# Fused attention and expert routing: attention's masks built first, more warm-up matmuls, the second q scaled in two halves, the sink gates planned later, and attention's order planned anew

## The chip, the cores and the metric

The kernel runs on one core of a Trainium2 chip. The metric is the device time of one execution in microseconds. Three runs of the kernel before are given, and beside them one profiled execution, from which all rows below come.

## The reference

The program is causal window attention followed by a mixture of experts. Shapes: 4 batches, 8 heads, 768 positions, 64 values per head; 3072 tokens of 512 values, 8 experts with 1024 hidden units.

```python
keep   = (pos < 4) | ((rel >= 0) & (rel < 128))       # rel = query position - key position
scores = where(keep, q @ k.T / 8, -1e9)
a      = exp(scores - max(scores)); a = a / (sum(a) + 1e-9)
x      = (a @ v), heads side by side                  # 3072 x 512
logits = x @ w_gate                                   # 3072 x 8
# greedy over all logits from the largest down: a token goes to its first expert
# that has fewer than 3072 / 8 = 384 tokens
out[tokens of e] = relu(x[tokens of e] @ w1[e]) @ w2[e]
```

## The kernel before

**Stages.** Attention runs first, over 24 chunks of 128 queries (4 batches of 6 blocks); it writes x to device memory and the logits into the tile `L`. Then the routing finds by counting, digit by digit, which tokens each expert takes, and each expert's tokens are gathered and go through the two matrix products. The change touches attention alone, and where the masks are made.

**One chunk of attention.** Chunk c needs its q (transposed, 64 values of two heads on the 128 partitions), its k behind the four sink keys, and its v. The steps, with the planner's names that the diff uses:

- q is scaled by 1/8: `qs` on GpSimd for a whole chunk (L74, called for one tile of 128x512), and `qs.0`, `qs.1`, `qs.2` on VectorE for the three pieces (heads 1/4, 1/4, 1/2) in which chunk 0 is loaded.
- `QK0` to `QK3` (L81, TensorE): scores of one head pair each, 260 columns (132 in the first block of a batch), two matmuls each in the program.
- `cp` (L86 to L88, VectorE): a predicated copy puts the sink and masked values in place. In the first block of a batch it writes `big` (-1e9) where the mask `m0` says so.
- `mx` (L91, VectorE) takes the negated maxima, `e` (L96, ScalarE) the exponentials with their sums.
- `T0`, `T1` (L102, TensorE) transpose the probabilities, `pe` (L103, ScalarE) copies them out, `A` and `B` (L104, L105, GpSimd) cut them to the window.
- `ss`, `sl` (L108, L109), `Ts` (L114), `pS` (L115): the probabilities of the sink keys, split in two parts, transposed and copied out.
- `AV0`, `AV1` (L122, TensorE): probabilities times v; `ae` (L129, VectorE) copies the result out.
- `X0`, `X1` (L137, L140, TensorE): the sinks' part, and the product that puts x and the gate's logits side by side; `xe` (L142, VectorE) divides by the sums and writes `xt`, `lm` (L144, VectorE) adds the logits up into `L`, and SyncE stores `xt` (L145).

**Sink gates.** `X0` multiplies the sink probabilities by a table `vx` that holds the sinks' values and their gate products. The table is made once, in the stretch of chunks 0 and 1: `U` (L62, TensorE, matmuls of 8 columns on the table `us`), `Uc` (ScalarE), `Us` (L67, TensorE, matmuls of 8 columns), `Ud` (L68, VectorE), then `vh` (L69), `vl` (L70), `vx` and `vy` (both L71, VectorE).

**Loads.** Tiles are loaded by DMAs that are issued on SP's queue and, for the q of chunks 0 and 1, on ScalarE's: the three pieces of chunk 0 with k and q in turn, then the identity and the q of chunk 1, then k and q of chunks 1 and 2, v of chunk 0, the sink tables, k and q of chunk 3. From then on a chunk's last score pair is followed by the loads of the chunk four ahead.

**Warm-ups.** `WARM0` matmuls of 512 columns on constants (L53) start TensorE; further ones, called `fill` (L151), stand where the planner sees TensorE idle for more than 400 ns.

**Masks.** GpSimd's queue begins with the routing's constants, written by the constructor of `Moe`. Behind them, in `attention`, stand the masks `mprev` and `m0` and the tile `big`, and behind these the scalings of q and the window cuts.

**Order.** No scheduler acts at run time: each engine runs its instructions in the order in which they are written. That order comes from a planner in the program. `table` lists each step with its engine, its cost in ns and the steps that it depends on; `buffers` says which tiles a step holds and until when; `schedule` plays this through and, on each engine, takes the ready step with the smallest priority, which is the chunk's number times a period plus an offset from the table `OFF`, among those that can start within a window of the earliest. `FIRST` holds the landing times that it assumes for the first loads, `COLD` the time up to which it takes TensorE's steps as 1.6 times as long, `SWITCH` what it adds between kinds of TensorE steps. Steps named `pr0` to `pr16` are the first part of the routing (L497 to L515 and the comparison L490, all on VectorE), done for the first 21 chunks beside the last three.

Of the kernel before, what the change touches and what calls it, by code (L numbers as in the profile page):

```python
# [15 lines left out]
def attention(ctx,tc,qd,kd,vd,vs,ud,pd,iwd,ident,idn,x_dram,L,side={}):  # L16
# [29 lines left out]
    mprev=tl([128,128],"mprev",I32); m0=tl([128,128],"m0",I32); one=tl([128,128],"one",I32); big=tl([128,128],"big")  # L46
    G.memset(one,1)
    for m in (mprev,m0): G.affine_select(m,one,[[1,128]],OP.is_gt,0,base=0,channel_multiplier=-1)
    G.memset(m0[:,0:4],1); G.memset(big,-1.0e9)
    m1=mprev[:,0:4]  # L50
# [23 lines left out]
    def op_qs(c,h=slice(0,HP),e=G): e.tensor_scalar(qs[c%NQ][:,h],qs[c%NQ][:,h],0.125,None,op0=OP.mult)  # L74
    def op_QK(c,g):

        i=c%NB; q=qs[c%NQ]; sp=T('p',c,f'QK{g}')
        k0=(i-1)*W+4 if i else 0; n=260 if i else 132
        for s in range(2):
            p=slice(64*s,64*s+64)  # L80
            PE.matmul(sp[:,s,:n],q[p,g,:],kk[p,g,k0:k0+n],start=True,stop=True)  # L81
# [75 lines left out]
UC=549; WARM0=5  # L157
# [32 lines left out]
def table(cfg):  # L190
# [5 lines left out]
    add('qs','P',lambda c: 1450 if c else None,[('ldq',0)])  # L196
    for h in range(4):
        add(f'QK{h}','E',lambda c: 435 if c%NB else 225,[('ldk',0),('ldk',-1),('qs',0),(f'qs.{min(h,2)}',0),(f'ldk{min(h,2)}',0)]+([(f'~QK{j}',-1) for j in range(3)] if h==3 else []))
        add(f'cp{h}','V',lambda c: 550 if c%NB==1 else 345,[(f'QK{h}',0)])
        add(f'mx{h}','V',344,[(f'cp{h}',0)])  # L200
        add(f'e{h}','A',697,[(f'mx{h}',0)])
# [12 lines left out]
    add('U','E',f0(860),[('ldu',0)])  # L214
# [34 lines left out]
def schedule(cfg,off,T,nb=NC,dl={}):  # L249
# [7 lines left out]
    for c in range(nb):  # L257
        for k,(e,cost,deps) in o.items():
            n=0
            for x,dc in deps:  # L260
                cc=c+dc
                if cc<0 or (dc<0 and cc//NB!=c//NB and x[0]!='~') or (x[0]=='^' and c==0): continue
                x=x.strip('~^')
                rdeps[x,cc].append((k,c)); n+=1
            nd[k,c]=n; ready[k,c]=0.0
# [92 lines left out]
COLD=6500  # L358
# [9 lines left out]
OFF={'A0': 15034, 'A1': 45179, 'AV0': 23765, 'AV1': 17217, 'B0': -9280, 'B1': -53066, 'QK0': -5907, 'QK1': -3388, 'QK2': -3032, 'QK3': -253, 'T0': 7878, 'T1': 10234, 'Ts': -92291, 'U': -35159, 'Uc': -39381, 'Ud': -42332, 'Us': 19706, 'X0': 32667, 'X1': 39254, 'ae0': 217110, 'ae1': -115057, 'cp0': -4377, 'cp1': 13457, 'cp2': -230461, 'cp3': -47449, 'e0': -61344, 'e1': 24247, 'e2': 10856, 'e3': 484225, 'lm': -15093, 'mx0': 32807, 'mx1': -73387, 'mx2': -8086, 'mx3': -51448, 'pS': -31001, 'pe0': -33445, 'pe1': -52676, 'pr0': -44011, 'pr1': 105836, 'pr10': 134063, 'pr11': 484687, 'pr12': -32310, 'pr13': 141140, 'pr14': 249747, 'pr15': 315275, 'pr16': 8621, 'pr2': -37615, 'pr3': 8456, 'pr4': -5323, 'pr5': -137567, 'pr6': -42400, 'pr7': 48263, 'pr8': 10969, 'pr9': 44553, 'qs': -85908, 'r': -21269, 'ra': 253505, 'sl': 96619, 'ss': 8175, 'vh': 287446, 'vl': 59670, 'vx': 316495, 'vy': 137937, 'xe': -83812, 'xo': -18776}  # L368
# [4 lines left out]
DL={}  # L373
# [483 lines left out]
def attention_moe(tc,qd,kd,vd,iwd,ident,w1,w2,out,n_sink,window,vs=None,ud=None,pd=None):  # L857
    nc=tc.nc
    with ExitStack() as ctx:
# [26 lines left out]
```

## Time and profile before

| what | value |
|---|---|
| three runs | 493.31, 495.43, 497.24 us; median 495.43 |
| profiled execution | 497.0 us, of which its span on the core is 495.3 |
| mean clock granted to TensorE in it | 0.968 |
| attention | from the start to about 155 us |
| routing and experts | from there to the end |

How to read it: the span begins with the first instruction of the core and ends with the last; the times of all rows are counted from its start. Where a line of the program holds one matmul of 4-byte values, the profile counts two or four for it, so the counts of its rows stand above those of the order. Rows that name a chain follow the execution back from its last instruction; a row of a timeline gives in brackets how long the engine stood idle ahead of it, and what ended that. Matmuls overlap, so that the mean duration of one is longer than the busy time divided by their count.

### The profile page before, as it was taken

Reading aid. Unit: us, or ns where it says so; the run is one execution under the profiler, and the core shown is the slowest. Engines: PE = TensorE matmul, PEld = TensorE weight load, DVE = VectorE, ACT = ScalarE, POOL = GpSimd, SP = SyncE. Lnnn points to the kernel's source line nnn. Section 1 sums busy time; section 2 is a strip of 40 time slices with the busy share of each in tenths; the row PEclk is TensorE's granted clock in tenths of the full one; section 3 lists DMA queues with packets and bytes.
Section 4 is the critical chain, followed back from the end, with each engine's and each line's share of the span. In section 5 each row is a group of like instructions: output and inputs, shape, how many; then the busy total and the mean of one; then the engine's idle time right before and its main releaser. Section 6 shows DMA issues by size and latency. Waiting matters only on the chain.

```text
span 495.3 us, 11327 instructions
## 1 busy us (share of the span) xinstructions
PE 468.7 (95%) x4147; PEld 386.4 (78%) x4147; DVE 379.8 (77%) x1147; ACT 234.0 (47%) x672; POOL 148.4 (30%) x212
## 2 busy tenths in 40 slices
PE   8999999999997698999989999999999999999994
PEld 4878787787786367867867877887888887998983
DVE  5699989899998687998989989999999374531210
ACT  4578887777870044344344353363523365522110
POOL 6667575665642010041022030301302142002001
PEclk9999999999998587999999999999999999999998
DMA  8656666766322171473562551745725674601001
GB/s 266 194 159 187 174 191 176 192 201 174 106 66 65 49 254 63 143 233 136 164 199 106 169 193 59 253 138 183 221 83 161 224 250 133 214 0 44 21 22 43
DMA packets 75464, 73.13 MB, mean 148 GB/s; under 512 B 28560, under 2 KB 57872, under 8 KB 75408
## 3 DMA queue, kind: packets, MB, share of 16 engines
q1 hardware_dynamic: 70992, 59.29, 39.7%
q0 software_dynamic: 3840, 12.59, 7.2%
q8 instruction: 33, 0.54, 0.4%
q10 hardware_dynamic: 576, 0.52, 0.4%
q14 instruction: 23, 0.19, 0.1%
HBM read 59.80 MB, written 12.58 MB: 146 GB/s over the span
## 4 chain that ended last, share of the span: by engine, by line
PE 61%; DVE 22%; DMA 8%; issue 4%; POOL 2%; ACT 1%; POOLq 0%; SPq 0%; DVEq 0%; ACTq 0%
PE ph L738 20%; PE py L751 15%; PE pp L81 8%; PE pp L122 6%; DVE wl L692 4%; PE pp L140 3%; DMA xg<-x_dram,idx 3%; DVE cmp L490 2%; DMA raw<-w 2%; PE pp L102 2%; DVE hl L743 2%; PE pr L562 2%; DMA out<-yo,idx 1%; DMA kk<-kd 1%; PE pt L704 1%
## 5 line engine op out<-in xcount | busy, mean ns | idle before, releaser
L690 ACT ACTIVATE wh<-raw 128x1024 fp32r<-128x1024 f32 x64 | 67.3, 1059 | 73.8 <-DMA raw<-w 46.4
L738 PE MATMUL ph<-xh,wh 128*128 128x384 f32 x256 | 92.1, 360 | 0.7 <-DVE hl L743 0.7
L692 DVE TENSOR_TENSOR wl<-raw,wh 128x1024 fp32r<-128x1024 f32 x64 | 77.9, 1218 | 12.9 <-ACT wh L690 12.5
L738 PE MATMUL ph<-xh,wl 128*128 128x384 f32 x256 | 87.1, 340 | 0.0
L738 PE MATMUL ph<-xl,wh 128*128 128x384 f32 x256 | 86.7, 342 | 0.2 <-DVE xl L727 0.2
L751 PE MATMUL py<-wh,hh 128*128 128x512 f32 x192 | 78.8, 411 | 0.0
L751 PE MATMUL py<-wl,hh 128*128 128x512 f32 x192 | 75.5, 393 | 0.0
L751 PE MATMUL py<-wh,hl 128*128 128x512 f32 x192 | 75.4, 393 | 0.0
L742 ACT ACTIVATE hh<-ph 128x384 fp32r<-128x384 f32 x64 | 31.3, 490 | 90.5 <-PE ph L738 82.0
L96 ACT ACTIVATE P<-pp,nmx 128x132 f32<-128x132 f32 x192 | 68.7, 371 | 9.1 <-DVE nmx L91 8.0
L756 POOL DMA_INDIRECT out<-yo,idx x24 | 24.9, 1038 | 153.6 <-ACT yo L754 119.5
L697 POOL DMA_INDIRECT xg<-x_dram,idx x24 | 29.0, 1209 | 123.1 <-DVE mx L505 34.2
L743 DVE SCALAR_TENSOR_TENSOR hl<-ph,hh 128x384 fp32r<-128x384 f32 x64 | 34.3, 549 | 39.3 <-ACT hh L742 39.2
L81 PE MATMUL pp<-kk,q 64*128 64x260 f32 (+1 forms) x384 | 61.1, 421 | 2.5 <-ACT P L96 1.0
L738 PEld LDWEIGHTS ph<-xh,wh 128*128 128x128 f32 x256 | 49.0, 192 | 4.3 <-DVE hl L743 2.2
L738 PEld LDWEIGHTS ph<-xh,wl 128*128 128x128 f32 x256 | 49.0, 192 | 1.2
L738 PEld LDWEIGHTS ph<-xl,wh 128*128 128x128 f32 x256 | 48.7, 191 | 0.7 <-DVE xl L727 0.5
L81 PEld LDWEIGHTS pp<-kk,q 64*128 64x128 f32 x384 | 33.9, 207 | 14.8 <-ACT P L96 7.5
L751 PEld LDWEIGHTS py<-wh,hl 128*128 128x128 f32 x192 | 36.0, 188 | 8.0
L91 DVE TENSOR_REDUCE nmx<-pp 128x2 f32<-128x264 f32 x96 | 39.8, 426 | 1.0
L751 PEld LDWEIGHTS py<-wh,hh 128*128 128x128 f32 x192 | 36.2, 188 | 5.2 <-ACT yo L754 0.2
L103 ACT ACTIVATE PT<-pp 128x512 f32<-128x512 f32 x48 | 28.7, 597 | 24.0 <-PE pp L102 19.8
(173 smaller groups left out, 824.6 us busy)
## 6 DMA issues: line engine op xcount, KB each, us to landing
raw<-w SPq DMA_DIRECT2D x64, 512.0 KB, 4.2
v<-vd SPq DMA_DIRECT2D x24, 256.0 KB, 3.3
x_dram<-xt SPq DMA_DIRECT2D x24, 256.0 KB, 3.0
kk<-kd SPq DMA_DIRECT2D x23, 264.0 KB, 4.2
q<-qd SPq DMA_DIRECT2D x22, 256.0 KB, 3.9
xg<-x_dram,idx POOLq DMA_INDIRECT x24, 4.0
out<-yo,idx POOLq DMA_INDIRECT x24, 3.2
us<-ud SPq DMA_DIRECT2D x1, 274.5 KB, 5.8
```

The lines of the kernel that those rows point to most:

```text
L81: PE.matmul(sp[:,s,:n],q[p,g,:],kk[p,g,k0:k0+n],start=True,stop=True)
L91: V.tensor_reduce(T('nmx',c)[:,2*g:2*g+2],sp[:,:,o:o+132],AX.X,OP.max,negate=True)
L96: A.activation(T('P',c)[:,4*s+g,:],sp[:,s,o:o+132],AF.Exp,bias=T('nmx',c)[:,h:h+1],scale=1.0,accum_out=T('sm',c)[:,h:h+1])
L103: def op_pe(c,g): A.activation(T('PT',c)[:,4*g:4*g+4,:].rearrange("p j (s n)->p s j n",s=2),T('p',c,f'T{g}')[:,:,0:256].rearrange("p s (j ...
L122: mm=PE.matmul(av[64*s:64*s+64,hp-2*g,:],T('v',j)[:,h*64:h*64+64],T(x,c)[:,h,:],start=hp==2*g and x=='A',stop=x=='B' or not i,skip_group_c ...
L690: g.add('A',947,lambda wh=wh,raw=raw: nc.scalar.activation(wh,raw,AF.Copy),[f'raw{n%4}'],[f'wh{s}'],f'H{k}.{j}',f'W{k}')
L692: g.add(e,{'V':1135,'P':2303}[e],lambda wh=wh,wl=wl,raw=raw,e=e: (nc.vector if e=='V' else nc.gpsimd).tensor_tensor(wl,raw,wh.bitcast(F32) ...
L697: g.add('P',1450,lambda t=t: nc.gpsimd.indirect_dma_start(out=self.xg[t],out_offset=None,in_=self.x_dram,in_offset=bass.IndirectOffsetOnAx ...
L738: for c,i in part: nc.tensor.matmul(p[:,0:CAP],three[i][0][:,c,:],three[i][1][:,c,:],start=n==0 and i==0,stop=last and i==2)
L742: g.add('A',371,lambda f=f,p=p: nc.scalar.activation(self.hh[:,f,:],p[:,0:CAP],AF.Relu),ps,[f'hh{f}'],f'hh{k}.{f}',f'H{k}')
L743: g.add('V',469,lambda f=f,p=p: nc.vector.scalar_tensor_tensor(self.hl[:,f,:],p[:,0:CAP],0.0,self.hh[:,f,:].bitcast(F32),op0=OP.max,op1=OP ...
L751: nc.tensor.matmul(p,x[:,f,ts],w,start=f==0 and i==0,stop=f==7 and i==2)
```

## The change

The masks move into a function of their own that is called before the routing's constants, so that GpSimd makes them first. Seven warm-ups stand at the start instead of five. The q of chunk 1 is scaled by two steps of two head pairs each, `qh0` and `qh1`, instead of one `qs`. In the planner's table `U` now waits for `AV1` of chunk 0, and costs 900; the fourth score pair of chunk 0 waits for `mx1` of chunk 0 (the mark `!` means: for chunk 0 alone); `COLD` is 7300. The table `OFF` has new values, and a table `DL` that was empty gives single steps of the chunks 0 to 2 and 20 to 23 an offset of their own.

```diff
+def attention_masks(nc,pool):
+    G=nc.gpsimd
+    mprev,m0,one=[pool.tile([128,128],I32,name=n) for n in ("mprev","m0","one")]; big=pool.tile([128,128],F32,name="big")
+    G.memset(one,1); G.memset(big,-1.0e9)
+    for m in (m0,mprev): G.affine_select(m,one,[[1,128]],OP.is_gt,0,base=0,channel_multiplier=-1)
+    G.memset(m0[:,0:4],1)
+    return mprev,m0,big
-def attention(ctx,tc,qd,kd,vd,vs,ud,pd,iwd,ident,idn,x_dram,L,side={}):
+def attention(ctx,tc,qd,kd,vd,vs,ud,pd,iwd,ident,idn,x_dram,L,masks,side={}):
...
-    mprev=tl([128,128],"mprev",I32); m0=tl([128,128],"m0",I32); one=tl([128,128],"one",I32); big=tl([128,128],"big")
-    G.memset(one,1)
-    for m in (mprev,m0): G.affine_select(m,one,[[1,128]],OP.is_gt,0,base=0,channel_multiplier=-1)
-    G.memset(m0[:,0:4],1); G.memset(big,-1.0e9)
-    m1=mprev[:,0:4]
+    mprev,m0,big=masks; m1=mprev[:,0:4]
...
+    def op_qh(c,g): op_qs(c,slice(2*g,2*g+2))
...
-UC=549; WARM0=5
+UC=549; WARM0=7
...
-    add('qs','P',lambda c: 1450 if c else None,[('ldq',0)])
+    add('qs','P',lambda c: 1450 if c>1 else None,[('ldq',0)])
+    for g in range(2): add(f'qh{g}','P',lambda c: 760 if c==1 else None,[('ldq',0)])
     for h in range(4):
-        add(f'QK{h}','E',lambda c: 435 if c%NB else 225,[('ldk',0),('ldk',-1),('qs',0),(f'qs.{min(h,2)}',0),(f'ldk{min(h,2)}',0)]+([(f'~QK{j}',-1) for j in range(3)] if h==3 else []))
+        add(f'QK{h}','E',lambda c: 435 if c%NB else 225,[('ldk',0),('ldk',-1),('qs',0),(f'qh{h//2}',0)]+([('!mx1',0)] if h==3 else [])+[(f'qs.{min(h,2)}',0),(f'ldk{min(h,2)}',0)]+([(f'~QK{j}',-1) for j in range(3)] if h==3 else []))
...
-    add('U','E',f0(860),[('ldu',0)])
+    add('U','E',f0(900),[('ldu',0),('AV1',0)])
...
-                if cc<0 or (dc<0 and cc//NB!=c//NB and x[0]!='~') or (x[0]=='^' and c==0): continue
-                x=x.strip('~^')
+                if cc<0 or (dc<0 and cc//NB!=c//NB and x[0]!='~') or (x[0]=='^' and c==0) or (x[0]=='!' and c): continue
+                x=x.strip('~^!')
...
-COLD=6500
+COLD=7300
...
+        masks=attention_masks(nc,top)
         m=Moe(ctx,tc,L,idn)
...
-            if n_sink==4 and window==128: attention(actx,tc,qd,kd,vd,vs,ud,pd,iwd,ident,idn,x_dram,L,m.side())
+            if n_sink==4 and window==128: attention(actx,tc,qd,kd,vd,vs,ud,pd,iwd,ident,idn,x_dram,L,masks,m.side())
```

Of the table `OFF` two entries show the kind of change: `'U': -35159` becomes `'U': -33562`, and `'Us': 19706` becomes `'Us': 1705`. Of `DL`, two are `'QK1@2': -6625` and `'T0@2': 8815`.

After the change the lines stand three to five further down: L62 becomes L65, L74 L77, L81 L85, L102 L106, L122 L126, L142 L146, L144 L148, L151 L155, and those of the routing from L490 on stand five further down.

**VectorE at its start.** The names are the q tile of chunk 0 (`q_0`), the score tiles (`pp`), the mask `m0` and the tile `big`, and the maxima (`nmx`). Before:

```order
L74 TENSOR_SCALAR q_0_181<-q_0_181 128x128 x2
L88 COPY_PREDICATED pp3_230<-m0_219,big_221 128x2x128
L74 TENSOR_SCALAR q_0_181<-q_0_181 128x256
L88 COPY_PREDICATED pp2_229<-m0_219,big_221 128x2x128
L91 TENSOR_REDUCE nmx_3_242<-pp3_230 128x2
```

After:

```order
L77 TENSOR_SCALAR q_0_190<-q_0_190 128x128 x2
L77 TENSOR_SCALAR q_0_190<-q_0_190 128x256
L92 COPY_PREDICATED pp3_230<-m0_64,big_66 128x2x128
L92 COPY_PREDICATED pp2_229<-m0_64,big_66 128x2x128
L95 TENSOR_REDUCE nmx_3_244<-pp3_230 128x2
```

The scaling of the third q piece (128x256) moves ahead of the first predicated copy.

**TensorE from the last scores of chunk 0 on.** `q_1` and `q_2` in a row are the q of the chunks 1 and 2, `idt` the identity of the transposes, `us` the table that L62 reads, `pk` the one that L67 reads, `A` and `v` the operands of A·V. Before:

```order
L81 MATMUL pp3_230<-kk_180,q_1_182 128x260 x2
L102 MATMUL pp2_229<-idt_62,P_2_238 128x64 x8
L81 MATMUL pp1_228<-kk_180,q_1_182 128x260 x2
L81 MATMUL pp0_227<-kk_180,q_1_182 128x260 x2
L62 MATMUL pp2_229<-us_186 128x8 x4
L102 MATMUL pp3_230<-idt_62,P_2_238 128x64 x8
L81 MATMUL pp2_229<-kk_180,q_1_182 128x260 x2
L114 MATMUL pp1_228<-idt_62,ss_2_258 128x64 x2
L81 MATMUL pp3_230<-kk_180,q_2_183 128x260 x2
L67 MATMUL pp1_228<-U_188,pk_187 128x8 x4
```

After:

```order
L85 MATMUL pp3_230<-kk_189,q_1_191 128x260 x2
L106 MATMUL pp2_229<-idt_62,P_2_240 128x64 x8
L85 MATMUL pp1_228<-kk_189,q_1_191 128x260 x2
L106 MATMUL pp0_227<-idt_62,P_2_240 128x64 x8
L85 MATMUL pp2_229<-kk_189,q_2_192 128x260 x2
L85 MATMUL pp3_230<-kk_189,q_2_192 128x260 x2
L85 MATMUL pp0_227<-kk_189,q_1_191 128x260 x2
L106 MATMUL pp1_228<-idt_62,P_1_239 128x64 x8
L85 MATMUL pp2_229<-kk_189,q_1_191 128x260 x2
L85 MATMUL pp1_228<-kk_189,q_2_192 128x260 x2
L126 MATMUL pp3_230<-A_2_254,v_4_216 64x128 x8
L65 MATMUL pp0_227<-us_195 128x8 x4
```

L62, which stood ahead of the second transpose of chunk 0, now stands behind the first A·V. The two transposes (L106) have one score pair between them. Ahead of this place the further warm-ups move: before, L151 issues two between the second and the third score pair of chunk 0; after, L155 issues four between the third and the fourth.

**VectorE in the last chunks.** `di`, `s`, `oh`, `w`, `mx`, `xb0`, `v`, `vm` and `f` are tiles of the routing's first part, `at` the copies of A·V, `ss` the split sink probabilities, `xt` the tile that is stored, `L` the logits. Before:

```order
L91 TENSOR_REDUCE nmx_2_241<-pp1_228 128x2
L511 TENSOR_SCALAR di_112<-s_101 128x21
L507 TENSOR_SCALAR di_112<-s_101 128x21
L506 TENSOR_SCALAR di_112<-s_101 128x21
L509 TENSOR_TENSOR oh_111<-w_110,mx_102 128x168
L508 CAST xb0_107<-di_112 128x42
L512 TENSOR_SCALAR di_112<-s_101 128x21
L129 COPY at_2_268<-pp2_229 128x256
L129 COPY at_1_267<-pp0_227 128x256 x2
L109 TENSOR_TENSOR ss_2_258<-P_1_237,ss_2_258 128x8x8
```

After:

```order
L146 TENSOR_TENSOR xt_2_273<-pp3_230,r_1_265 128x2x4x72
L113 TENSOR_TENSOR ss_1_259<-P_0_238,ss_1_259 128x8x8
L148 TENSOR_REDUCE L_61<-xt_2_273 128x8
L146 TENSOR_TENSOR xt_1_272<-pp0_227,r_0_264 128x2x4x72
L502 TENSOR_REDUCE v_107<-L_61 128x21
L148 TENSOR_REDUCE L_61<-xt_1_272 128x8
L506 TENSOR_TENSOR w_119<-L_61,v_107 128x168
L504 TENSOR_TENSOR vm_108<-pen_103,v_107 128x21
L133 COPY at_2_270<-pp1_228 128x256
L507 TENSOR_SCALAR f_109<-vm_108 128x21
L508 TENSOR_TENSOR w_119<-w_119,rev_95 128x168
```

Before, a run of routing steps stood ahead of the copies of A·V and of the split; after, the split stands ahead of the first routing step, and the copies come sooner among those steps.

## Rows read from the trace of the kernel before

**Rows 1.** Windows by stage, all engines: length, busy us of each engine, granted clock, DMA.

```profile
9.00:19.00 10.00, 10.00 (x64) 7.96 (x62) 6.93 (x23) 6.79 (x32) 5.63 (x5) 1.00 1.10 349
...
27.00:151.00 124.00, 120.42 (x1766) 99.78 (x1763) 117.46 (x347) 95.11 (x418) 75.26 (x99) 1.00 0.59 162
...
156.00:177.00 21.00, 15.36 (x188) 8.80 (x189) 15.58 (x79) 2.11 (x2) 4.99 (x11) 0.51 0.30 90
```

**Rows 2.** Timeline of VectorE, the last L144 of attention: start us, us, instruction, idle.

```profile
154.74 0.27 DVE L144 TENSOR_REDUCE L<-xt 128x8 f32<-128x64 f32 x1
```

**Rows 3.** Groups by form, 8 to 22.8 us: count | busy us, mean ns | idle.

```profile
L81 PE MATMUL pp<-kk,q 64*128 64x260 f32 x28 | 7.9, 688 | 0.7 <-DMA kk<-kd 0.7
...
L102 PE MATMUL pp<-idt,P 64*128 64x64 f32 x32 | 2.7, 318 | 0.0
...
L122 PE MATMUL pp<-A,v 128*64 128x128 f32 x16 | 2.0, 428 | 0.0
...
L62 PE MATMUL pp<-us 128*128 128x8 f32 x8 | 1.9, 363 | 0.0
```

**Rows 4.** The same view, 27 to 151 us.

```profile
L81 PE MATMUL pp<-kk,q 64*128 64x260 f32 x276 | 43.2, 412 | 0.1
...
L102 PE MATMUL pp<-idt,P 64*128 64x64 f32 x342 | 18.0, 223 | 1.2 <-DVE xt L142 1.0 <-ACT P L96 0.2
```

**Rows 5.** Chain that ended last: start us, us, what ran or was waited for.

```profile
2.89 5.02 DMA kk<-kd
...
27.47 1.97 PE pp L122 x32
```

**Rows 6.** Timeline of TensorE, the first 23 us.

```profile
0.85 2.29 PE L53 MATMUL pp<-const-float32-0.0 128*128 128x512 bf16 x5 [0.85 <-PEq L879]
3.77 1.29 PE L81 MATMUL pp<-kk,q 64*128 64x132 f32 x8 [0.62 <-DVE q L74]
4.99 1.04 PE L151 MATMUL pp<-const-float32-0.0 128*128 128x512 bf16 x2
...
8.05 1.24 PE L81 MATMUL pp<-kk,q 64*128 64x260 f32 x4 [0.74 <-DMA kk<-kd]
...
20.95 1.97 PE L122 MATMUL pp<-A,v 128*64 128x128 f32 x16
```

**Rows 7.** Line 533 alone: min/median/max ns, first and last start.

```profile
L533 PE MATMUL ph<-onesb x21: 326/527/528, 171.6 to 178.3; 128*128 128x384 bf16 x21
```

**Rows 8.** Timeline of TensorE: warm-up matmuls of the routing stage.

```profile
171.59 5.85 PE L533 MATMUL ph<-onesb 128*128 128x384 bf16 x19
```

**Rows 9.** Timeline of VectorE, the start.

```profile
5.38 0.43 DVE L88 COPY_PREDICATED pp<-m,big 128x256 f32<-128x256 int32 x1 [1.20 <-POOL big L49]
5.72 0.28 DVE L74 TENSOR_SCALAR q<-q 128x256 f32<-128x256 f32 x1
```

**Rows 10.** Timeline of ScalarE with its DMA queue, the start.

```profile
0.82 1.84 ACTq L29 DMA_DIRECT2D q<-qd  x4
```

**Rows 11.** DMA issues of 0 to 3 us: KB each, median us to landing.

```profile
q<-qd ACTq DMA_DIRECT2D x1, 128.0 KB, 3.4
```

**Rows 12.** Timeline of GpSimd, the start.

```profile
6.29 1.50 POOL L74 TENSOR_SCALAR q<-q 128x512 f32<-128x512 f32 x1 [0.94 <-DMA q<-qd]
9.52 1.49 POOL L74 TENSOR_SCALAR q<-q 128x512 f32<-128x512 f32 x1 [1.73 <-DMA q<-qd]
```

**Rows 13.** Timeline of VectorE: the second L142.

```profile
31.95 0.76 DVE L142 TENSOR_TENSOR xt<-pp,r 128x576 f32<-128x576 f32 x1
```

**Rows 14.** VectorE alone, first copy of chunk 1 to that L142: window, busy us.

```profile
9.40:31.95 22.55, 17.80 (x50) 1.00 0.63 192
```

**Rows 15.** Timeline of TensorE, the last chunks.

```profile
147.85 0.40 PE L137 MATMUL pp<-vx,pS 64*128 64x288 f32 x2 [0.30 <-DVE at L129]
...
149.08 0.28 PE L114 MATMUL pp<-idt,ss 64*128 64x64 f32 x2 [0.43 <-DVE ss L109]
```

More of the change, by code (lines that the diff above doesn't have):

```diff
@@ L367, in plan_of @@
     return dict(seq=[(k,c) for _,_,k,c in ev],slot=sl,bufs={t:n for t,(n,_) in buffers(cfg).items()})
-OFF={'A0': 15034, 'A1': 45179, 'AV0': 23765, 'AV1': 17217, 'B0': -9280, 'B1': -53066, 'QK0': -5907, 'QK1': -3388, 'QK2': -3032, 'QK3': -253, 'T0': 7878, 'T1': 10234, 'Ts': -92291, 'U': -35159, 'Uc': -39381, 'Ud': -42332, 'Us': 19706, 'X0': 32667, 'X1': 39254, 'ae0': 217110, 'ae1': -115057, 'cp0': -4377, 'cp1': 13457, 'cp2': -230461, 'cp3': -47449, 'e0': -61344, 'e1': 24247, 'e2': 10856, 'e3': 484225, 'lm': -15093, 'mx0': 32807, 'mx1': -73387, 'mx2': -8086, 'mx3': -51448, 'pS': -31001, 'pe0': -33445, 'pe1': -52676, 'pr0': -44011, 'pr1': 105836, 'pr10': 134063, 'pr11': 484687, 'pr12': -32310, 'pr13': 141140, 'pr14': 249747, 'pr15': 315275, 'pr16': 8621, 'pr2': -37615, 'pr3': 8456, 'pr4': -5323, 'pr5': -137567, 'pr6': -42400, 'pr7': 48263, 'pr8': 10969, 'pr9': 44553, 'qs': -85908, 'r': -21269, 'ra': 253505, 'sl': 96619, 'ss': 8175, 'vh': 287446, 'vl': 59670, 'vx': 316495, 'vy': 137937, 'xe': -83812, 'xo': -18776}
+OFF={'A0': 3566, 'A1': 68904, 'AV0': 23490, 'AV1': -54870, 'B0': 50180, 'B1': -8375, 'QK0': -11402, 'QK1': -6817, 'QK2': -7324, 'QK3': 208, 'T0': 3441, 'T1': 6408, 'Ts': -24063, 'U': -33562, 'Uc': 36180, 'Ud': -33378, 'Us': 1705, 'X0': 28046, 'X1': -11706, 'ae0': 22354, 'ae1': 12933, 'cp0': -60932, 'cp1': -113859, 'cp2': 36173, 'cp3': 118185, 'e0': 14705, 'e1': -236202, 'e2': 42795, 'e3': -147363, 'lm': -69786, 'mx0': -207103, 'mx1': -20852, 'mx2': -175794, 'mx3': -57270, 'pS': 13167, 'pe0': 628292, 'pe1': -41356, 'pr0': 14452, 'pr1': 10874, 'pr10': 26429, 'pr11': 67741, 'pr12': 103900, 'pr13': 35733, 'pr14': 58646, 'pr15': -237999, 'pr16': -37794, 'pr2': -22384, 'pr3': 21144, 'pr4': 36050, 'pr5': 132677, 'pr6': 622285, 'pr7': 201632, 'pr8': -14661, 'pr9': 1836, 'qh0': 0, 'qh1': 3896, 'qs': 45199, 'r': 564000, 'ra': 435238, 'sl': 421755, 'ss': 732629, 'vh': 49536, 'vl': 108950, 'vx': -6186, 'vy': 779306, 'xe': -58979, 'xo': 107970}
 PCFG={'win': 80, 'ae': 'V'}
```

2 lines of the change are left out of this document (1 added, 1 removed).

## Prediction

> **What bounds the kernel now.** I read the stages first. TensorE is busy 120.4 of 124 us between 27 and 151 us and VectorE 117.5, so attention, which ends at 155.0 us (154.74 + 0.27), is bound by both together [rows 1, 2]. The change touches nothing behind it but the time at which it ends. I then looked for a stage in which the same work takes longer, and compared groups by form. From 8 to 22.8 us 28 score matmuls of 260 columns keep TensorE busy for 7.9 us (0.282 each), against 43.2 for 276 (0.157 each) later on; transposes take 0.084 against 0.053 [rows 3, 4]. The 16 matmuls of the first A·V take 1.97 us; later 32 of them take 1.97 [rows 5, 6].
>
> So TensorE runs at the lower of its two levels (1.2 GHz) until about 23 us. The clock column does not say so: it shows 1.00 there, though nothing ran at that speed. The durations do: five warm-ups of 512 columns in 2.29 us are about 1.1 columns per ns, and the same 384-column matmul takes 527 ns in a stretch at a granted 0.51 and 326 at full clock [rows 1, 6, 7]. That is what the change can win back. What did TensorE do before a rise? From 171.6 us on it ran 19 warm-ups without a break, and came out fast [rows 7, 8]. At about 23 us it had run scores, transposes and the first A·V in one piece [rows 6]. What did not raise it: 0.85 to 8 us, with breaks of 0.62 and 0.74, and 8 to 19 us, without a break, but with sixteen matmuls of the sink gates in it (8 columns each, 1.9 us for every eight) [rows 1, 3, 6].
>
> The Trainium skill ("TensorE: Matmul & The Clock Gate", Part 1) says that the array starts throttled and that sustained matmul activity releases it. The trace disagrees with that as it stands: TensorE is busy 10.00 of 10 us from 9 to 19 and stays slow [rows 1, 3]. By the rule alone nothing would be left to win there, and the sum would be the rival "nothing but the tail" below, 496.5.
>
> **The change, part by part.** The profiled execution took 497.0 us, its span 495.3; the sum is made against 497.0. That is 1.6 above the median of the runs shown, 495.43, and inside their spread.
>
> *Masks first.* VectorE waited 1.20 us for `big` and made its first predicated copy at 5.38 [rows 9]. Now GpSimd writes the masks before the routing's constants, which nobody reads until the last chunks. But the order also puts the scaling of the third q piece ahead of that copy on VectorE. Its DMA is the third of four issued within 1.84 us from 0.82 on, so at about 1.73, and lands 3.4 later, at 5.1 [rows 10, 11]. With 0.28 for the scaling [rows 9] the copy starts at about 5.4, as before: **0.0** (bounds -0.1 and +0.3). A transfer takes the place of the wait. Behind that copy in VectorE's queue stand the other copies of chunk 0, for which the exponentials wait; they keep their times.
>
> *Seven warm-ups, and four later.* Two more at 0.46 (2.29/5) fill the break of 0.62 in front of the first scores; the first two pairs end at about 5.3. The two warm-ups that stood at 4.99 are gone from there, so a break of some 0.3 opens before the third pair, which needs the scaling that ends at 5.4. Four (1.8 us) now stand between the third and the fourth pair, about 6.3 to 8.1 [rows 6]. They lie over the wait for k of chunk 1, issued at 2.89 and landing at 7.9 [rows 5], so they cost nothing; if that transfer came earlier, up to 1.8. What then breaks the stretch before the first A·V is the 0.3 and perhaps a moment before q of chunk 2, whose scaling on GpSimd ends at 9.52 + 1.49 = 11.0 [rows 12].
>
> *q in halves.* The first half would be ready at 6.29 + 0.75 = 7.04 instead of 7.79 [rows 12]; k comes at 7.9, so **0.0**. SP's queue keeps its loads; only the first two stores of xt move, and nobody waits for them before the routing.
>
> *Sink gates later.* Line 62's matmuls move behind the first A·V, line 67's further still. The first L142 now waits for them together with more of the score work, but the second L142, which stood at 31.95 us, has the same steps ahead of it in both orders on TensorE, and on VectorE the same 46 but for one tiny one [rows 13]. I take that instruction as the mark.
>
> *What the clock gives back.* If the upper level comes by about 8 to 11 us instead of 23, TensorE saves: scores 7.9 - 28 x 0.157 = 3.5; transposes 2.7 - 32 x 0.053 = 1.0; A·V 2.0 - 1.0 = 1.0; sink gates, of which no row shows the upper level, between 0 and half of 3.8, and by the ratio of the scores (0.157/0.282) 1.7. Sum 7.2, bounds 5.5 and 7.4 [rows 3 to 6]. Not all of it can come back. VectorE is in order and has 17.80 us of work from the first copy of chunk 1 at 9.40 to the mark [rows 14]; that copy waits for k of chunk 1 and cannot come earlier. With no idle time the mark would stand at 27.2 (4.75 won); with the share of 117.5/124 that VectorE reaches in the steady stretch [rows 1] it takes 18.8, so 28.2: 3.8 won. The early chunks have more waits, not fewer, so I take the latter: **-3.8**, bounds 0 and -4.75 by this row, -7.2 if VectorE's time shrank too.
>
> *The middle of attention.* From chunk 4 on the plan swaps neighbours (a third score pair ahead of a second and the like) at a pace that the same two engines set: **0.0**, bounds -1 and +1, the size by which 120.4 and 124 leave room [rows 1].
>
> *The last chunks.* Before, steps of the routing's preparation stood ahead of the copies of A·V and of the split of the sink weights on VectorE, and TensorE waited 0.30 and 0.43 for them [rows 15]. Now the split stands ahead of the first of them, the two copies of one chunk have two or three of them ahead instead of six, and the eight ahead of the next copy lie beside the A·V that this copy waits for. **-0.5**, bounds 0 and -0.7.
>
> Sum: 497.0 - 3.8 - 0.5 = 492.7.
>
> **Rivals.** *The clock rises only behind the first A·V.* For it: that is what stood ahead of the rise before [rows 6]; against it: eleven warm-ups now stand in the first 8 us with hardly a break, and warm-ups alone did it at 171.6 [rows 8]. Then seven score groups, three transposes and A·V are as slow as before, and only the sink gates and one transpose gain: 1.7 + 0.25, with the tail 2.4 in all: 494.6. The Trainium skill ("TensorE: Matmul & The Clock Gate", Part 4: PE-mode transpose) says that transposes do not count towards the clock as matmuls do; two of them now stand close together early, one score pair apart. That would make this rival likelier; no row here shows transposes alone.
>
> *All of it comes back.* VectorE's 17.80 us hold instructions stretched by waits for GpSimd, and a different order may shed them: 497.0 - 7.2 - 0.5 = 489.3.
>
> *Slower: the sink gates right behind A·V.* The stretch that raised the clock before ran on from A·V into scores. Now line 62's matmuls of 8 columns follow A·V at once, and line 67's after a few groups. If the early warm-ups do not raise the clock and this breaks the later stretch, it stays low through the second A·V: four more score groups (4 x 4 x 0.125 = 2.0) and 32 matmuls of A·V (2.0) are slow. 497.0 + 4.0 - 0.5 = 500.5. It decides from the moment at which the first A·V ends at the lower level.
>
> *Nothing but the tail.* Part of the spread of the runs before may be a clock that sometimes rose early; if it does not rise earlier now, 496.5.
>
> **How the numbers follow.** About 1%, 5 us, is what a measurement of this kernel can tell from no change, that is below 490.5 or above 500.4. Forecast 0.58, with its own range 491.2 to 494.2; behind A·V 0.20; all back 0.12; slower 0.06; tail alone 0.04. The range 489.4 to 496.5 takes in all but the slower case and the fringe of "all back". Faster by over 1%: the 0.12 and 0.05 of the forecast's lower fringe, 0.17; slower 0.05; the rest 0.78.
>
> **What would show it.** In the changed profile: the first predicated copy at 5.4 with no wait for `big` but with one for a q DMA; score groups of about 0.157 us per matmul from 11 us on; line 62 behind the first A·V; the second L142 near 28 us; the last L144 ending near 150.7; no wait of TensorE for lines 129 and 109 in the last chunks. The forecast is wrong if scores are still at 0.28 us each at 15 us, or if the second L142 stands where I say and the end of attention does not follow it.

## The result, and the profile after

The changed kernel takes 490.33 us (median of 20 runs, 486.83 to 493.6) against 495.32 (20 runs, 491.52 to 498.22): a ratio of 0.9907, 95% interval 0.9881 to 0.9933, so 3.3 to 5.9 us. 490.33 lies in the stated range, 489.4 to 496.5, though under the forecast's own, 491.2 to 494.2. The ratio is that of the means of the runs within 1.5% of the fastest of their kernel, here and below, and so differs a little from the quotient of the medians, which are of all runs. The middle of the ratio is just under 1% faster, the case that had 0.78; the median, 490.33, is just below the 490.5 of the case that had 0.17. The result lies on the line between the two.

The profiled execution took 491.29 us, its span 489.6. The stages, with the columns of [rows 1]:

```profile
9.00:19.00 10.00, 8.69 (x90) 5.88 (x91) 8.88 (x27) 7.77 (x39) 7.63 (x8) 1.00 1.08 341
...
27.00:149.00 122.00, 118.74 (x1741) 98.27 (x1738) 113.95 (x337) 92.10 (x408) 73.71 (x99) 1.00 0.59 160
```

The steady stretch runs as before: TensorE is busy 118.7 of 122 us, before 120.4 of 124 [rows 1]. What changed lies ahead of it. The groups by form of the same 8 to 22.8 us as in [rows 3]:

```profile
L85 PE MATMUL pp<-kk,q 64*128 64x260 f32 x44 | 6.9, 422 | 0.4 <-ACT P L100 0.3
...
L65 PE MATMUL pp<-us 128*128 128x8 f32 x8 | 1.1, 259 | 0.0
```

44 score matmuls take 6.9 us there, 0.157 each, which is the figure of [rows 4] and not the 0.282 of [rows 3]; the eight of the sink gates take 1.1 us instead of 1.9. The timeline of TensorE, beside [rows 6]:

```profile
0.85 3.15 PE L56 MATMUL pp<-const-float32-0.0 128*128 128x512 bf16 x7 [0.85 <-PEq L885]
...
6.19 0.81 PE L85 MATMUL pp<-kk,q 64*128 64x132 f32 x4 [1.01 <-DVE pp L92]
6.93 1.89 PE L155 MATMUL pp<-const-float32-0.0 128*128 128x512 bf16 x4
8.75 1.44 PE L85 MATMUL pp<-kk,q 64*128 64x132 f32 x8
...
10.27 0.66 PE L85 MATMUL pp<-kk,q 64*128 64x260 f32 x4
...
16.11 1.09 PE L126 MATMUL pp<-A,v 128*64 128x128 f32 x16
17.14 1.06 PE L65 MATMUL pp<-us 128*128 128x8 f32 x8
```

Up to 9.8 us the lower level (1.2 GHz) still shows: four matmuls of 132 columns take 0.81 us and the four later warm-ups 1.89. From 10.27 a score group takes 0.66, the first A·V 1.09 instead of 1.97, and the sink gates stand behind it. The trace's records of the granted clock begin at 9.8 us, before at 23.3. The timeline of VectorE:

```profile
5.14 0.30 DVE L77 TENSOR_SCALAR q<-q 128x256 f32<-128x256 f32 x1 [1.22 <-DMA q<-qd]
5.35 0.76 DVE L92 COPY_PREDICATED pp<-m,big 128x256 f32<-128x256 int32 x2
...
9.61 0.43 DVE L92 COPY_PREDICATED pp<-m,big 128x256 f32<-128x256 int32 x1 [1.67 <-PE pp L85]
...
10.43 0.42 DVE L90 COPY_PREDICATED pp<-mprev,pp 128x256 f32<-128x256 int32 x1
...
28.60 0.75 DVE L146 TENSOR_TENSOR xt<-pp,r 128x576 f32<-128x576 f32 x1
...
151.93 0.43 DVE L148 TENSOR_REDUCE L<-xt 128x8 f32<-128x64 f32 x2
```

The first predicated copy starts at 5.35 behind the scaling of the third q piece, which waited 1.22 us for its DMA; `big` holds nobody. Up to 9.61 VectorE sat idle for 1.67 us until the last scores of chunk 0 came, and those stood behind the four warm-ups; the first copy of chunk 1 followed at 10.43. The second L146 stands at 28.60 (31.95 in [rows 13]), 3.35 us earlier; the last L148 ends at 152.36 (155.01 by [rows 2]), 2.65 earlier. The profiled pair differs by 5.7 us, so 3.05 of them arise behind attention. There the code is the same. Windows of the routing and the first expert, before and then after, clock in the third column from the right:

```profile
187.10:194.00 6.90, 6.07 (x24) 5.66 (x25) 5.59 (x16) 4.08 (x6) 0.00 (x0) 0.51 0.24 80
194.00:201.00 7.00, 7.00 (x48) 5.97 (x48) 5.58 (x18) 0.49 (x1) 0.00 (x0) 1.00 0.01 2
```

```profile
184.00:191.00 7.00, 6.21 (x43) 5.43 (x44) 6.70 (x21) 4.30 (x7) 0.00 (x0) 1.00 0.29 79
191.00:198.00 7.00, 6.92 (x47) 5.69 (x46) 6.48 (x22) 0.98 (x2) 0.00 (x0) 1.00 0.17 61
```

The kernel before fell to the lower level once more, from 187.1 to 194.0 us, with the first expert's matrix products under way; the changed one did not. That this goes by chance and not by the kernel, the six profiles of whole kernels suggest (the last two columns from the timelines and the records of the granted clock):

| kernel | from the last logits step to the end, us | at the lower level in it, up to 300 us |
|---|---|---|
| changed, gates early | 335.4 | 17.1 |
| before, two warm-ups | 336.1 | 20.5 |
| before, gates late | 336.6 | 23.9 |
| changed | 337.2 | 20.5 |
| before | 340.3 | 27.3 |
| changed, no late warm-ups | 342.1 | 30.7 |

The same code takes 335 to 342 us there, in the main longer the longer the clock is low, and the two kernels stand on both sides. So eight of the experiments leave routing and experts out.

### The profile page after: what moved, and what is told of

Read it like the earlier page. It is cut to its first block, busy times and chain, and to the rows that moved or that the text cites. A ratio compares the mean times of both kernels' runs of the same rounds, so it can differ in the third digit from the quotient of the medians.

```text
span 489.6 us, 11364 instructions
## 1 busy us (share of the span) xinstructions
PE 462.1 (94%) x4151; PEld 379.3 (77%) x4151; DVE 377.9 (77%) x1147; ACT 233.3 (48%) x672; POOL 148.6 (30%) x213
## 4 chain that ended last, share of the span: by engine, by line
PE 55%; DVE 27%; DMA 7%; issue 5%; ACT 3%; POOL 1%; POOLq 0%; ACTq 0%; DVEq 0%; SPq 0%
PE ph L743 18%; PE py L756 16%; PE pp L85 6%; PE pp L126 5%; DVE wl L697 4%; DMA xg<-x_dram,idx 4%; DVE cmp L495 3%; PE pp L144 2%; ACT P L100 2%; DVE nmx L95 2%; DVE hl L748 2%; DVE pp L90 2%; PE pp L106 2%; PE pr L567 2%; POOL xg L702 1%
## 5 line engine op out<-in xcount | busy, mean ns | idle before, releaser
L743 PE MATMUL ph<-xh,wh 128*128 128x384 f32 x256 | 90.8, 355 | 0.7 <-DVE hl L748 0.6
L743 PE MATMUL ph<-xh,wl 128*128 128x384 f32 x256 | 86.1, 336 | 0.0
L702 POOL DMA_INDIRECT xg<-x_dram,idx x24 | 29.0, 1208 | 120.4 <-DVE mx L510 31.3
L85 PE MATMUL pp<-kk,q 64*128 64x260 f32 (+1 forms) x384 | 57.6, 403 | 2.6 <-ACT P L100 1.3
L85 PEld LDWEIGHTS pp<-kk,q 64*128 64x128 f32 x384 | 32.1, 195 | 14.7 <-ACT P L100 8.2
L108 POOL TENSOR_SCALAR_AFFINE_SELECT A<-PT 128x512 f32<-128x512 f32 x48 | 30.4, 636 | 38.7 <-ACT PT L107 38.6
```

The costliest lines, as they stand in the source:

```text
L108: def op_A(c,g): G.affine_select(T('A',c)[:,4*g:4*g+4],T('PT',c)[:,4*g:4*g+4],[[0,4],[1,128]],OP.is_ge,0.0,base=0,channel_multiplier=-1)
L702: g.add('P',1450,lambda t=t: nc.gpsimd.indirect_dma_start(out=self.xg[t],out_offset=None,in_=self.x_dram,in_offset=bass.IndirectOffsetOnAx ...
L743: for c,i in part: nc.tensor.matmul(p[:,0:CAP],three[i][0][:,c,:],three[i][1][:,c,:],start=n==0 and i==0,stop=last and i==2)
```

## The experiments

Times are medians with range and count. The first four are whole kernels, beside 35 runs of the kernel before with a median of 495.14.

**1. The kernel before with two more warm-ups ahead of chunk 1.**

```diff
+            if (k,c)==('QK0',1):
+                for j in range(2): PE.matmul(T('p',1,'QK0')[:,0,:],wz[:,0:128],wz,start=True,stop=True)
             ops[k[:-1]](c,int(k[-1]))
```

> The kernel before, with two more warm-up matmuls of 512 columns between the last score pair of chunk 0 and the first of chunk 1, so that TensorE runs without a break from the fills at 4.99 us to the sink gates at about 11.5; nothing else. Theory (the clock came back early because warm-ups and scores ran without a break ahead of the sink gates, and that is most of the gain): score matmuls at 0.157 us each before 12 us, the second L142 at 28.5 to 29.5 us instead of 31.95, attention ending 2.5 to 3.5 us earlier, the time 2 to 4 us below before. Rival (the order is the gain, the sink gates' place above all): the clock still rises near 23 us, the second L142 at about 32, the time within 1 us of before.

494.37 us (489.21 to 497.65, 12), ratio 0.9974 (0.9936 to 1.0012). The timeline of TensorE:

```profile
7.66 1.01 PE L157 MATMUL pp<-const-float32-0.0 128*128 128x512 bf16 x2 [0.34 <-ACT P L96]
...
12.04 1.87 PE L62 MATMUL pp<-us 128*128 128x8 f32 x8
...
21.50 1.97 PE L122 MATMUL pp<-A,v 128*64 128x128 f32 x16
```

The theory fell. TensorE ran without a break from 7.66 on, and the gates (1.87) and the first A·V at 21.50 (1.97) are as slow as in [rows 3, 6]; the second L142 stands at 32.55, the level rose at 23.9, and the time is within 1 us of before, as the rival said. In this profile an unbroken stretch that soon holds the sink gates did not bring the level.

**2. The changed kernel without the four later warm-ups.**

```diff
-            for j in range(c[1]): PE.matmul(d,wz[:,0:128],wz,start=True,stop=True)
+            for j in range(0): PE.matmul(d,wz[:,0:128],wz,start=True,stop=True)
```

> The changed kernel without the four warm-ups of L155 between the third and the fourth score pair of chunk 0; the seven at the start stay. Theory (these four close the break in which TensorE waited for k of chunk 1, and so bring the upper level at 9.8): the breaks are open again, the level comes behind 12 us, the second L146 stands at 29.5 to 31 us instead of 28.60, the time 1 to 3 us above the changed kernel. Rival (the seven at the start do it): scores at 0.157 us from 10 us on, the second L146 at 28.6, the time as that of the changed kernel.

492.64 us (488.62 to 495.48, 12), ratio to before 0.9955 (0.9922 to 0.9987), 2.3 above the changed kernel. Timeline and windows:

```profile
3.93 0.72 PE L85 MATMUL pp<-kk,q 64*128 64x132 f32 x8
...
7.52 1.24 PE L85 MATMUL pp<-kk,q 64*128 64x260 f32 x4 [1.68 <-POOL q L77]
```

```profile
3.90:7.30 3.40, 1.47 (x17) 1.05 (x16) 2.68 (x8) 1.41 (x9) 2.16 (x20) 1.00 1.04 312
7.30:10.80 3.50, 3.28 (x26) 2.70 (x28) 2.50 (x9) 2.97 (x15) 3.29 (x5) 0.51 1.08 368
```

Both theories were half right. In this profile seven warm-ups alone had the level up by 3.9 us: eight matmuls of 132 columns take 0.72 instead of 1.29 [rows 6]. Then TensorE sat idle for 1.68 us, and from 7.3 to 10.8 the clock is down again. Here the four would have had to hold the level, not to raise it; in the changed kernel's own profile it came only behind them, at 9.8, so that they may also raise it. Their absence also let chunk 1 start at 7.52: the second L146 stood at 26.63, and the last L148 ended at 148.69, 3.67 earlier than in the profile with them. The routing then took the 342.1 of the table. So the 2.3 of the medians can hold some of the routing's scatter; experiment 7 leaves the routing out.

**3. The kernel before with the gates behind the first A·V.**

```diff
-    add('U','E',f0(860),[('ldu',0)])
+    add('U','E',f0(860),[('ldu',0),('AV1',0)])
```

> The kernel before with one edit of the planner's table: the sink gates' first step waits for the first A.V; warm-ups and masks as before, the order otherwise nearly that of before. Theory (the early sink gates, matmuls of 8 columns, were what kept TensorE at the lower level through 11 to 20 us): the level rises between 11 and 16 us, the second L142 at 29 to 30.5, the time 1 to 3 us below before. Rival (only warm-ups in the first 10 us bring the early rise): rise near 23 us as before, the second L142 at 31.5 to 32.5, the time within 1 us of before. Slower by 3 to 4 us if the gates behind A.V keep the level low.

495.25 us (493.14 to 498.24, 12), ratio 1.0022 (0.9988 to 1.0056). The timeline of TensorE:

```profile
13.69 0.53 PE L102 MATMUL pp<-idt,P 64*128 64x64 f32 x8
...
17.13 1.09 PE L122 MATMUL pp<-A,v 128*64 128x128 f32 x16
```

With five warm-ups as before, the level did rise sooner, at 13.9 (a transpose group of 0.53 us at 13.69, A·V in 1.09), and the second L142 stood at 29.30, 2.65 earlier, both as the theory had it. Nothing of it arrived: the last L144 begins at 155.2, before at 154.74 [rows 2]. Experiment 11 takes that up.

**4. The changed kernel with the gates early.**

```diff
-    add('U','E',f0(900),[('ldu',0),('AV1',0)])
+    add('U','E',f0(900),[('ldu',0)])
```

> The changed kernel with one edit of the planner's table undone: the sink gates' first step no longer waits for the first A.V, so that it stands ahead of the second block of scores again; warm-ups, masks and halves as changed. Theory (the level is up at 9.8, ahead of the gates in either place): no change of level, the gates at about half of their 1.9 us, the second L146 within 0.7 us of 28.6, the time within 1 us of the changed kernel. Rival (the place of the gates is what is won): the level low until about 20 us, the second L146 at 31 or later, the time 2 to 4 us above the changed kernel.

492.12 us (490.99 to 495.87, 12), ratio to before 0.9976 (0.9947 to 1.0005), 1.8 above the changed kernel, between the two theories' figures. In its profile the level stayed up, the first eight matmuls of the gates took 1.03 us and the second L146 stood at 28.13, as the theory said. The loss is at the end: this edit of the table also moved steps of the last chunks. VectorE there, this kernel and then the changed one:

```profile
150.10 0.85 DVE L495 TENSOR_TENSOR cmp<-xb,row 128x1344 bf16<-128x1344 bf16 x1
150.86 0.32 DVE L514 TENSOR_TENSOR oh<-w,mx 128x168 bf16<-128x168 f32 x1
151.11 0.74 DVE L133 COPY at<-pp 128x256 f32<-128x256 f32 x2
...
153.53 0.27 DVE L148 TENSOR_REDUCE L<-xt 128x8 f32<-128x64 f32 x1
```

```profile
148.69 0.41 DVE L133 COPY at<-pp 128x256 f32<-128x256 f32 x1
149.02 0.85 DVE L495 TENSOR_TENSOR cmp<-xb,row 128x1344 bf16<-128x1344 bf16 x1
149.79 0.42 DVE L133 COPY at<-pp 128x256 f32<-128x256 f32 x1
```

The copies of the last A·V (L133) stand at 151.11 behind the routing steps L510, L495 and L514, together 1.3 us; in the changed kernel one stands ahead of the long comparison and one behind it. From the 18th L148 to the last it takes 31.04 us against 29.36.

**5 to 8. Attention alone.** The cut is the same in all of these and the last four:

```diff
-        m.pools(ctx,w1,w2,x_dram,out)
-        with tc.manual_schedule(engines=set(ENGS[:5])): m.run()
+        nc.sync.dma_start(out[0:128,0:NC*E],L.rearrange("p c e->p (c e)"))
```

> The kernel before, cut off behind attention: routing and experts are left out, and in their place the logits tile is stored into the first rows of the output. Attention is unchanged. It measures attention alone, 156 to 160 us by the profile before (155.0 us, the store and what lies around the span), in many runs. Theory (the scatter of the whole kernel, 490 to 499 us, comes mostly from the clock in the routing, which is left out here): the runs lie within 4 us of each other. Rival (it comes from attention): they scatter by 6 us or more.

> The changed kernel, cut off behind attention in the same way: routing and experts are left out. Theory A (the whole 5 us of the medians are won in attention): its median 4 to 5.5 us below that of the kernel before cut in the same way. Theory B (the profiled pair is typical, attention wins about 2.65 and the rest of that pair's difference was the clock in the routing): 2 to 3.3 us below.

> The changed kernel cut off behind attention (routing and experts are left out), without the four warm-ups of L155. Theory (they cost nothing and hold the clock up): its median 1 to 3 us above the changed kernel cut in the same way. Rival (they push the first scores of chunk 1 from 7.5 to 9.4 us, as in its profile, and the clock comes back anyway): 1 to 3 us below it.

Its edit is that of experiment 2. The last of the four:

```diff
-    for i in range(WARM0): PE.matmul(pp[0][:,0],wz[:,0:128],wz,start=True,stop=True)
+    for i in range(WARM0+2): PE.matmul(pp[0][:,0],wz[:,0:128],wz,start=True,stop=True)
```

> The kernel before cut off behind attention (routing and experts are left out), with seven warm-ups at the start instead of five and its own order otherwise. Theory (seven at the start alone can bring the upper level at about 4 us, and the early order does not matter for it): its median 2 to 4 us below the kernel before cut in the same way. Rival (the breaks and the sink gates behind them bring the lower level back, or it never comes): within 0.7 us of it, the scores at 0.28 us each at 15 us.

| cut kernel | median us (range, runs) | level up by | second L142/L146 |
|---|---|---|---|
| 5, before | 159.99 (157.47 to 161.52, 6) | 20.6 | 30.97 |
| 6, changed | 156.50 (155.22 to 157.54, 6) | 9.3 | 27.93 |
| 7, changed, no late warm-ups | 157.57 (157.24 to 158.36, 6) | 4.9, then down 8.3 to 15.1 | 28.03 |
| 8, before, seven warm-ups | 159.22 (158.0 to 162.13, 6) | 4.4, then twice down | 30.44 |

Attention alone wins 3.5 us by the medians, between theories A (4 to 5.5) and B (2 to 3.3) and inside the whole kernel's interval. Six runs a side are few: their means differ by 3.25, with a 95% interval of 1.7 to 4.8, which shuts out neither theory. In the two profiles the last logits step ends 3.9 apart. The remaining 1.5 of the whole medians can be chance in the routing; no run settles it. Cut, the six runs of the kernel before still spread by 4.05 us, between the theory's 4 and the rival's 6, against 8.2 for 35 whole runs. Without the later warm-ups attention is 1.07 slower, as the theory had it (by the means 1.3, interval 0.3 to 2.3). Seven warm-ups alone win 0.8, about what the rival said, and the ranges do not tell it from nothing. Windows of that kernel:

```profile
7.90:11.30 3.40, 3.28 (x20) 2.29 (x20) 2.37 (x7) 2.51 (x13) 1.71 (x3) 0.51 1.08 359
11.30:14.70 3.40, 3.02 (x28) 2.06 (x26) 2.85 (x11) 3.07 (x16) 1.10 (x3) 1.00 1.10 352
14.70:21.50 6.80, 6.80 (x52) 5.75 (x50) 4.32 (x13) 4.51 (x21) 5.27 (x6) 0.50 0.74 236
```

The level comes at 4.4, goes at 7.9 in the breaks of TensorE, comes back at 11.3 and goes again at 14.7, right behind the first sink gates at 11.39, until 21.5. The order after the start is that of before, and what was won at the second L142 (0.53) is there at the end (0.8).

**9 to 12. Parts undone and parts alone** (beside these the whole kernel before took 495.5, beside the four above 497.5, so that differences between the two groups carry some of its scatter). First masks behind the constants and q of chunk 1 whole:

```diff
-        masks=attention_masks(nc,top)
         m=Moe(ctx,tc,L,idn)
+        masks=attention_masks(nc,top)
...
-    add('qs','P',lambda c: 1450 if c>1 else None,[('ldq',0)])
-    for g in range(2): add(f'qh{g}','P',lambda c: 760 if c==1 else None,[('ldq',0)])
+    add('qs','P',lambda c: 1450 if c else None,[('ldq',0)])
+    for g in range(2): add(f'qh{g}','P',lambda c: None,[('ldq',0)])
```

> The changed kernel cut off behind attention (routing and experts are left out), with two parts undone: the masks made behind the routing's constants again, and the second q scaled whole. The order is otherwise that of the changed kernel. Theory (both are worth nothing: the first copy waits for the third q piece anyway, and the first scores of chunk 1 stand behind the four warm-ups, not behind the scaling): the first predicated copy within 0.4 us of 5.35, the second L146 within 0.5 us, the median within 0.8 us of the changed kernel cut in the same way (156.5). Rival (the masks are what the warm-ups cannot hide): 1 to 2 us above it.

156.68 us (155.51 to 160.03, 6) against 156.50: no difference that shows. VectorE's first copy, and TensorE:

```profile
5.49 0.77 DVE L92 COPY_PREDICATED pp<-m,big 128x256 f32<-128x256 int32 x2 [0.23 <-POOL m L21]
```

```profile
5.74 1.04 PE L155 MATMUL pp<-const-float32-0.0 128*128 128x512 bf16 x4
...
8.09 0.71 PE L85 MATMUL pp<-kk,q 64*128 64x260 f32 x4 [0.88 <-DMA kk<-kd]
```

The copy starts at 5.49 instead of 5.35, now waiting 0.23 for the mask. Here the level was up sooner, the four warm-ups took 1.04 and TensorE then waited 0.88 for k of chunk 1: with the level up they do lie in the shadow of that transfer.

**10. The four warm-ups split, two on either side of the last score pair**, by the edit of experiment 1 and `range(2)` in place of `range(c[1])`.

> The changed kernel cut off behind attention (routing and experts are left out), with the four later warm-ups split: two ahead of the last score pair of chunk 0 and two behind it, ahead of the first pair of chunk 1. Theory (the four hold the last copy of chunk 0 back, and VectorE stood idle for 1.67 us there, at the start of a stretch that VectorE sets): that copy 0.7 to 0.9 us earlier, the second L146 and the end 0.4 to 0.9 us earlier, the median 0.3 to 1 us below 156.5. Rival (VectorE then waits for the scores of chunk 1 instead, which start as before): the second L146 and the median within 0.3 us.

155.68 us (155.3 to 157.22, 5), 0.8 lower, but the ranges overlap, and its second L146 at 27.21 is only 0.17 ahead of that of experiment 9, where the level also rose early (the 0.7 to experiment 6 is the later rise there). Its TensorE:

```profile
7.22 0.59 PE L161 MATMUL pp<-const-float32-0.0 128*128 128x512 bf16 x2 [0.41 <-DMA kk<-kd]
...
11.09 1.59 PE L85 MATMUL pp<-kk,q 64*128 64x260 f32 x12 [1.30 <-POOL q L77]
```

What holds the next scores is q of chunk 2, whose scaling on GpSimd they wait for 1.30 us. The split is not shown to help.

**11. The clock's parts on the old tables:** experiments 1, 3 and 8 together.

> The kernel before cut off behind attention (routing and experts are left out), with only those parts of the change that touch the clock: seven warm-ups at the start, two more ahead of the first scores of chunk 1, and the planner's edit by which the sink gates wait for the first A.V. Masks, q of chunk 1 and the tables of offsets as before. Theory (the clock is nearly all of the gain, and warm-ups and gates are both needed for it): scores at 0.157 us by 12 us at the latest and no lower level from then to the end of attention, the median 2.5 to 3.8 us below the kernel before cut in the same way (159.99), near 156.5. Rival (the new tables of offsets are needed too): 159 or more.

160.77 us (160.19 to 162.3, 5): no gain on 159.99, though the level was up from 3.9 us on but for 21.0 to 24.4. VectorE's fifth, 18th and last L144, this kernel and then the kernel before cut in the same way:

```profile
48.87 0.26 DVE L144 TENSOR_REDUCE L<-xt 128x8 f32<-128x64 f32 x1
...
123.54 0.26 DVE L144 TENSOR_REDUCE L<-xt 128x8 f32<-128x64 f32 x1
...
154.27 0.27 DVE L144 TENSOR_REDUCE L<-xt 128x8 f32<-128x64 f32 x1
```

```profile
50.97 0.27 DVE L144 TENSOR_REDUCE L<-xt 128x8 f32<-128x64 f32 x1
...
124.23 0.27 DVE L144 TENSOR_REDUCE L<-xt 128x8 f32<-128x64 f32 x1
...
153.82 0.27 DVE L144 TENSOR_REDUCE L<-xt 128x8 f32<-128x64 f32 x1
```

At the fifth it leads by 2.10, at the 18th by 0.69, at the end it trails by 0.45. The edit of the table lets the planner put other steps first all through the later chunks, and with that order 1.4 is lost in the middle and 1.1 in the last chunks. The 1.1 is sure: from the 18th step to the last it takes 29.6 us in all four profiles with the order of before and 30.7 in both with this edit (experiments 3 and 11). The 1.4 is less so: from the fifth to the 18th the four take 72.99 to 74.14, the two 74.67 and 75.28. So the rival stands: without tables that fit, an early clock does not reach the end. The converse, the new tables with the clock low as before, was not measured; what the order is worth by itself stays open.

**12. The changed kernel, cut, with the gates early**, by the edit of experiment 4.

> The changed kernel cut off behind attention (routing and experts are left out), with the planner's wait of the sink gates for the first A.V taken away, so that they stand between the first scores again. Theory (with the warm-ups the level is up in time, and the gates' place only shifts the order): the median within 0.8 us of 156.5. Rival (early gates at the upper level are followed by a fall, as at 14.7 us in the kernel before with seven warm-ups): the lower level again in the records between 12 and 25 us, the median 1 to 3 us above 156.5.

159.74 us (158.23 to 161.5, 5), 3.2 above the changed kernel. The gates in TensorE's timeline, and windows:

```profile
11.07 1.03 PE L65 MATMUL pp<-us 128*128 128x8 f32 x8 [1.01 <-DMA us<-ud]
```

```profile
5.30:12.10 6.80, 5.21 (x48) 3.24 (x46) 5.27 (x17) 5.30 (x26) 4.40 (x6) 1.00 1.04 331
12.10:15.50 3.40, 3.40 (x22) 2.39 (x22) 1.66 (x5) 1.19 (x6) 1.76 (x3) 0.50 1.07 348
```

The gates stand at 11.07; from 12.1 to 15.5 the clock is down, as the rival said. But the fall does not account for the 3.2. The profile is of the slowest run, 161.5. The run of 159.74 has a mean clock of 0.991, which leaves about 2.8 us at the lower level in all of it, less than this fall of 3.4 us; and in the profile of experiment 4, with the same order, the level stayed up. Against the profile of experiment 6 the last logits step ends 5.04 later: the second L146 is 1.46 later (29.39), the stretch from there to the 18th step takes 1.9 more, and the last chunks lose the 1.7 of experiment 4 again. Only these 1.7 are shown to be order.

## Why the prediction was right, step by step

**The bound and the clock.** Right. The scores of the first chunks were slow because TensorE ran at 1.2 GHz, the level came at 9.8 instead of 23.3, within the forecast's 8 to 11, and eight matmuls of the gates take 1.1 us, the saving that the ratio of the scores gave (1.7 of 3.8). -3.8 was forecast, a second L146 near 28.2: it stands at 28.60, -3.35, in the profiled pair and at -3.04 in the cut pair. Attention whole wins 2.65 and 3.9 in these pairs, 3.5 by the cut medians, against 4.3 forecast with the tail. How much of it is the clock alone is not shown: with an early clock on the old tables (experiment 11) the second L142 was 1.11 ahead and the fifth logits step 2.10. Nor need the level be up early for the mark to gain: in the profile of experiment 7 it was down from 8.3 to 15.1, and the second L146 still stood at 28.03, 2.94 ahead of the cut kernel before.

That the mark came so near is in part luck. The forecast let VectorE start chunk 1 at 9.40 and take 18.8 us to the mark for 17.80 us of work. It started at 10.43 and took 18.17, with 16.99 us of work in them: 1.03 lost, 0.6 won. Nor does k hold that copy at 9.40, as the forecast had it: it comes at 8.47 to 8.91 in six profiles of variants of the changed kernel, all with the level up by 5.5 us, and in experiment 2 the mark, at 26.63, stands below the 27.2 that the forecast gave for no idle time.

**What failed in that step** is "they cost nothing" of the four warm-ups, which the wait for k was to cover until 7.9. At the lower level the fourth ended at 8.82, with the last scores of chunk 0 still behind it, and kept VectorE idle until 9.61. Part of this is a break that was put at 0.3: ahead of the third score pair TensorE waited 1.01. Which level they meet differs from run to run: seven warm-ups had it up between 3.9 and 5.4 us in eight of ten profiles, at 9.3 and 9.8 in two. With the level up they take 1.04 and are hidden (experiment 9).

**Masks and halves**: 0.0 and 0.0 were forecast, and 0.2 measured for both together, not told apart from nothing; a q transfer took the place of the wait, as said.

**Sink gates later.** The forecast counted this as part of the clock's return; what it missed is that their place and the tables go together. Experiments 3 and 11 moved them on the old tables and lost later what they won early.

**The middle.** 0.0 was forecast, within 1 either way. From the second mark to the 18th logits step the changed order took 0.94 more than before in the profiled pair and 0.65 less in the cut pair; six profiles of the changed order take 92.45 to 94.27 us there, so that nothing finer than the bounds can be told. With the tail this is why the last logits step ended at 152.36 and not near 150.7: 0.4 at the mark, 0.9 here, 0.3 in the last chunks.

**The last chunks.** -0.5 was forecast. From the 18th logits step to the last it took 29.58 us (the last at 154.74 [rows 2]) and takes 29.36: -0.2, inside the bounds. The two waits of [rows 15] are gone, but the comparison (0.85 at 149.02) still stands between copies. That this place can cost is shown by the 31.04 of experiment 4.

**The base.** The sum started from an execution 1.7 above the median of its kernel, which held a fall of the clock at 187.1, by chance as far as the table shows. 492.7 landed 2.4 above the measured median mostly for that: the same terms from 495.32 give 491.0.

**The rivals.** "Behind the first A·V" fell: with seven warm-ups the level was up ahead of it at some time in all ten profiles, and with five in experiment 3. "Tail alone" fell too. "All of it comes back" was 7.7 us in attention, and 2.65 to 3.9 came. The slower case did not come: in the changed kernel the gates at 17.14 and 20.14 run at the upper level, and no fall follows. A fall behind gates does occur, though: where they stand among the first scores (experiments 8 and 12), and once behind the first A·V, at 21.0 in experiment 11. The Trainium skill ("TensorE: Matmul & The Clock Gate", Part 1) says that sustained activity releases the throttle; the warm-ups bear it out, while experiment 1 ran unbroken from 7.66 to 21 us and stayed low.

## What to carry to other kernels

Look for a cold stretch by comparing the same group in two stages, not by the clock column alone, and close the breaks behind the warm-ups as well as the one ahead of them. In a kernel with an order planned whole, judge a local win at the end of the stage: one wait added to the table shifted steps 20 chunks on and gave the win back. Where a later stage scatters by more than the effect, cut the kernel behind the stage in question.

## What was not expected of the hardware

The level went as easily as it came: behind a break of 1.68 us (experiment 2), and in three profiles soon after matmuls of 8 columns that ran at the upper level (at 12.1, 14.7 and 21.0 us). In eight other profiles such matmuls ran at the upper level and no fall came in attention behind them, so that they are not shown to be the cause. And the routing, the same code in every kernel, took 335.4 to 342.1 us, in the main by how long the clock was low in it.
